# One code copy for the tokens of an expert beyond 512, behind all experts, in a kernel of attention, MLP and mixture of experts

## The chip, the cores and the metric

The kernel runs on one core of a Trainium2 chip, in one launch. Times are device microseconds (us) of that core. The kernel before takes 1265.66 us in the median of three runs (1262.17 to 1268.53). The engines are TensorE (PE in the profile; PEld is its weight load, which overlaps the matmuls), VectorE (DVE), ScalarE (ACT), GpSimd (POOL) and SyncE (SP). Each engine has its own instruction stream, and waits for others by semaphores. A branch stands in the stream of every engine, since all of them must go the same way.

## The reference, cut to what matters

Three stages follow each other on float32 data. The first is attention with batch 4, 8 heads, 576 positions and 64 columns a head, in which each query keeps its 32 largest scores:

```
scores = q @ k.T / 8
mask   = scores >= (32nd largest of the row)
attn   = softmax of the kept scores;  x = attn @ v       # 2304 tokens x 512
```

The second is a gated MLP with a root-mean-square norm, 512 to 1536 and back to 512:

```
xn = x / sqrt(mean(x*x) + 1e-6) * rms_g
x  = (silu(xn @ w_gate) * (xn @ w_val)) @ w_out
```

The third, which the change touches, is a mixture of 8 experts. Each token goes to the one expert with its largest logit:

```
logits = x @ w_gate + modality_bias[modality_id];  e_idx = argmax(logits)
gate_w = softmax(logits)[e_idx]
for e in range(8):                                    # tokens of expert e
    out[mask] = gate_w[mask] * (relu(x[mask] @ w1[e]) @ w2[e])   # 512 -> 1024 -> 512
```

How many tokens an expert gets is known only when the kernel has computed the logits. The weights of one expert are 4 MB, 32 MB for all.

## The kernel before, in words

The function front(False) holds attention, MLP and gate, some 930 us, in an order of steps written out by hand. It leaves three things: the rows x2_d in device memory, a table tab_d with the numbers and gate weights of each expert's tokens, and cnt_i, the eight counts. It also computes bad_i, a count of values outside the range in which the fast arithmetic holds; under "If bad > 0" (lines 1102 to 1103) the whole front is there again in exact arithmetic, and all engines jump over it. The last vector work before that is in verdict2 (lines 977 to 983), which writes cnt_i and bad_i.

Then come the experts, one after another (loop over e, from line 1262). The unit of work is 256 tokens (UNIT). For one unit

- gather (line 1135) reads 256 rows of the table (idx, six kept) and fetches the tokens' rows by an indirect DMA from POOL into xg, of which there are three buffers;
- columns (line 1146) transposes them on TensorE (line 1154, eight transposes a unit) and splits each value into a high part xh (ScalarE) and a low part xl (VectorE), as TensorE multiplies the rounded parts;
- hidden (line 1165) makes the first product, 8 blocks of 12 matmuls with 256 columns (lines 1177), and the ReLU, again split into hh and hl;
- emit (line 1220) makes the second product, two halves of 24 matmuls with 512 columns (line 1230), scales by the gate weight (line 1235) and scatters 128 rows at a time by an indirect DMA from POOL (line 1236).

One such unit has 32 matmuls xh times wh at line 1177. The weights come in pieces of 512 KB on SP's queue (load_piece, line 1115) and are split into high and low parts by ScalarE and VectorE (split, line 1125).

The first unit of an expert is always computed, also where it is not full. While it runs, the next expert's weights are loaded and split, and the next tokens gathered and transposed: the code asks for them at chosen points of hidden and emit (lists later, between, ahead). Behind it comes what depends on the count. "If counts > 256" (line 1289) holds the second unit, either whole or, where at most 128 tokens are left, as a half (line 1290, hidden_half at line 1189). "If counts > 512" (line 1294) holds a loop over all units beyond (line 1295), with its own gather, transposes, hidden and emit. It needs the expert's weights in the buffers, so it stands ahead of the next expert. Tokens of the next expert's first unit are gathered ahead of these branches.

The order of instructions on each engine is set when the program is built: a scheduler orders the instructions between two branches by a simulated time line. Nothing moves across a branch or across the end of an If or a loop, but the lists above let the next expert's work stand inside the present one's.

Of the kernel before, what the change touches and what calls it, by code (L numbers as in the profile page):

```python
# [20 lines left out]
def topk_attention_swiglu_moe_kernel(  # L21
# [97 lines left out]
    tok = const.tile([128, NB], I32, name="tok")  # L119
    cnt_i = const.tile([128, E], I32, name="cnt_i")  # L120
    bad_i = const.tile([128, 1], I32, name="bad_i")
    ssall = const.tile([128, NB], F32, name="ssall")


# [85 lines left out]
    def front(exact):  # L210
# [766 lines left out]
        def verdict2(pt, ones, b_):  # L977

            nc.tensor.matmul(out=pt[:, 16:16 + E], lhsT=ones16, rhs=acc_oh, start=True, stop=True)
            nc.vector.tensor_copy(cnt_i, pt[:, 16:16 + E])  # L980
            if not exact:
                nc.tensor.matmul(out=pt[:, 8:9], lhsT=ones, rhs=b_, start=True, stop=True)
                nc.vector.tensor_copy(bad_i, pt[:, 8:9])
# [151 lines left out]
    def gather(rows, queue=nc.gpsimd):  # L1135
        idx = up.tile([128, 2, 2], I32, name="idx", tag="idx", bufs=6)
        queue.dma_start(out=idx, in_=tab_d[rows, :].rearrange("(j p) t -> p j t", j=2))
        xg = up.tile([128, 2, DM], F32, name="xg", tag="xg", bufs=3)
        for j in range(2):
            last["gather"] = nc.gpsimd.indirect_dma_start(  # L1140
                out=xg[:, j, :], out_offset=None, in_=x2_d,
                in_offset=bass.IndirectOffsetOnAxis(ap=idx[:, j, 0:1], axis=0), bounds_check=NT, oob_is_err=False,
            )
        return idx, xg

    def columns(u):
        idx, xg = u
        xh = up.tile([128, KD, UNIT], F32R, name="xh", tag="xh", bufs=3)
        xl = up.tile([128, KD, UNIT], F32R, name="xl", tag="xl", bufs=3)
        for kk in range(0, KD, 2):  # L1150
            pt = ps_g.tile([128, 512], F32, name="pg")
            for a in range(2):
                for j in range(2):
                    nc.tensor.transpose(
                        pt[:, a * 256 + j * 128:a * 256 + (j + 1) * 128],
                        xg[:, j, (kk + a) * 128:(kk + a + 1) * 128], ident,
                    )
            pv = pt.rearrange("p (a n) -> p a n", a=2)
            nc.scalar.copy(out=xh[:, kk:kk + 2, :], in_=pv)
            nc.vector.tensor_tensor(  # L1160
                out=xl[:, kk:kk + 2, :], in0=pv, in1=xh[:, kk:kk + 2, :].bitcast(F32), op=OP.subtract
            )
        return idx, xh, xl

    def hidden(ws, u, between=()):
        idx, xh, xl = u
        between = list(between)
        hh = up.tile([128, KF2, UNIT], F32R, name="hh", tag="hh", bufs=1)
        hl = up.tile([128, KF2, UNIT], F32R, name="hl", tag="hl", bufs=1)
        for m in range(KF2):  # L1170
            pt = ps_h.tile([128, UNIT], F32, name="ph")
            n = 0
            for kk in range(KD):
                wh, wl = ws[kk]
                fs = slice(m * 128, (m + 1) * 128)
                for l, r in ((wh, xh), (wh, xl), (wl, xh)):
                    nc.tensor.matmul(out=pt, lhsT=l[:, fs], rhs=r[:, kk, :], start=(n == 0), stop=(n == 3 * KD - 1))  # L1177
                    n += 1
            a = nc.scalar.activation(out=hh[:, m, :], in_=pt, func=AF.Relu)  # L1179
            d = nc.vector.scalar_tensor_tensor(  # L1180
                out=hl[:, m, :], in0=pt, scalar=0.0, in1=hh[:, m, :].bitcast(F32), op0=OP.max, op1=OP.subtract
            )
            if between:
                with tc.issue_after(a.ins), tc.issue_after(d.ins):
                    for fn in between.pop(0):
                        fn()
        return idx, hh, hl
# [32 lines left out]
    def emit(ws, u, between=None, halves=2):  # L1220
        idx, hh, hl = u
        for j in range(halves):
            pt = ps_u.tile([128, 512], F32, name="pu")
            n = 0
            js = slice(j * 128, (j + 1) * 128)
            for f in range(KF2):
                wh, wl = ws[NPC + f // 2]
                ds_ = slice((f % 2) * DM, (f % 2 + 1) * DM)
                for l, r in ((hh, wh), (hh, wl), (hl, wh)):
                    nc.tensor.matmul(out=pt, lhsT=l[:, f, js], rhs=r[:, ds_], start=(n == 0), stop=(n == 3 * KF2 - 1))  # L1230
                    n += 1
            if j == 0 and between:
                between()
            o = up.tile([128, DM], F32, name="o", tag="o", bufs=2)
            nc.scalar.activation(out=o, in_=pt, func=AF.Copy, scale=idx[:, j, 1:2].bitcast(F32))  # L1235
            nc.gpsimd.indirect_dma_start(  # L1236
                out=out, out_offset=bass.IndirectOffsetOnAxis(ap=idx[:, j, 0:1], axis=0),
                in_=o, in_offset=None, bounds_check=NT - 1, oob_is_err=False,
            )
# [22 lines left out]
    for e in range(E):  # L1262
        more = e + 1 < E
        wn = []
        box = {}
        later = []
        for i in range(NPC):
            later.append([lambda i=i: split(ws[NPC + i])])
            if e == 0:
                later[i] += [lambda i=i: load_piece(wn, 1, 2 * i, nc.scalar), lambda i=i: load_piece(wn, 1, 2 * i + 1, nc.scalar)]  # L1270
        if more:
            with tc.issue_after(first) if e == 0 else ExitStack():
                g1 = gather(rows(e + 1, 0))
            if e > 0:
                for i in range(2 * NPC):
                    load_piece(wn, e + 1, i)
        later.append([lambda: box.update(c2=columns(g2))])

        def ahead():
            for w in wn[0:NPC]:  # L1280
                split(w)

        if more:
            later += [[]] * (KF2 - 1 - len(later)) + [[ahead]]
        emit(ws, hidden(ws, c1, later), (lambda: box.update(c1=columns(g1))) if more else None)
        c2, c1 = box["c2"], box.get("c1")
        if more:
            g2 = gather(rows(e + 1, 1))
        with tc.If(counts[e] > UNIT):
            with tc.If(counts[e] > UNIT + 128) as whole:  # L1290
                emit(ws, hidden(ws, c2))
            with whole.Else():
                emit(ws, hidden_half(ws, c2), halves=1)
        with tc.If(counts[e] > 2 * UNIT):  # L1294
            with tc.For_i(2 * UNIT, counts[e], UNIT) as i:
                emit(ws, hidden(ws, columns(gather(bass.ds(e * NT + i, UNIT)))))
        if more:
            ws = wn


# [31 lines left out]
```

## Time and profile before

| | |
|---|---|
| median of three runs | 1265.66 us |
| the profiled execution | 1265.35 us, its span 1263.7 us |
| mean granted clock of TensorE | 0.929 |
| TensorE matmuls, busy | 1140.6 us |
| VectorE, busy | 927.7 us |
| ScalarE, busy | 833.3 us |
| POOL, busy | 738.8 us |
| moved by DMA | 87.80 MB |

The profile is one execution. Its span runs from the first to the last record; the 1.65 us around it belong to the run's time. Busy time does not count branches, register loads, semaphores or the issue of a DMA: where an engine stands in a branch it is idle in these figures, and the engine's sequencer has an entry of its own (PEq, POOLq). Matmuls are handed over to TensorE ahead of time, so its sequencer can stand in a branch while earlier matmuls still run. The experts fill the last 325 us of the span. Times of the timeline are counted from the start of the span.

### The profile page before, as it was taken

The page shows a single profiled execution, that of the slowest core. Times are in us where ns is not written, and L with a number is a line of the kernel's source. Part 1 is how long each engine was busy: PE and PEld are TensorE (multiplying, and loading weights), DVE is VectorE, ACT ScalarE, POOL GpSimd, SP SyncE. Part 2 cuts the span into 40 slices and gives each one's busy share as a digit, 9 for nine tenths or more (in the row PEclk, how much of TensorE's full clock was granted, in tenths as well). Part 3 has the DMA queues.
Part 4 walks back from the last instruction along what each step waited for, and adds up shares of the span by engine and source line. Part 5 has one row for each costly group of instructions (what it writes and reads, how often), then busy time and mean ns, then how long its engine had stood idle before and what let it go on. Part 6 is the DMA issues. An engine that isn't in the chain of part 4 may idle for free. (4 is left out here: it accounts for less than half of the span.)

```text
span 1263.7 us, 32277 instructions
## 1 busy us (share of the span) xinstructions
PE 1140.6 (90%) x12286; PEld 1044.3 (83%) x12286; DVE 927.7 (73%) x2883; ACT 833.3 (66%) x1757; POOL 738.8 (58%) x850
## 2 busy tenths in 40 slices
PE   6976777989999999999999999999948898999985
PEld 6965667988999999999898999999937897798884
DVE  7999999669999999999999999921115434254251
ACT  5868888677888888888998788753315434354251
POOL 7866767668857888777798767643423222022120
PEclk9856677989999999999999999999978998999998
DMA  8143312011000111000011000000029525354130
GB/s 289 51 126 84 96 44 79 14 45 48 9 17 17 28 40 53 17 8 18 23 38 40 17 15 10 2 11 19 2 71 348 185 73 209 109 184 139 70 116 18
DMA packets 68894, 87.80 MB, mean 69 GB/s; under 512 B 34386, under 2 KB 43734, under 8 KB 68696
## 3 DMA queue, kind: packets, MB, share of 16 engines
q1 hardware_dynamic: 60152, 63.66, 16.3%
q0 software_dynamic: 6320, 16.31, 3.8%
q10 hardware_dynamic: 2224, 5.25, 1.2%
q8 instruction: 117, 1.92, 0.7%
q14 instruction: 81, 0.66, 0.2%
HBM read 75.58 MB, written 10.92 MB: 68 GB/s over the span
## 5 line engine op out<-in xcount | busy, mean ns | idle before, releaser
L561 DVE MAX8 w<-w 128x8 f32<-128x296 f32 x576 | 249.8, 456 | 1.2
L595 POOL TENSOR_TENSOR s<-s,r 128x576 f32<-128x576 f32 x144 | 201.2, 1419 | 31.8 <-ACT r L591 31.5
L564 DVE MATCH_REPLACE8 w<-w 128x296 f32<-128x296 f32 x432 | 193.1, 449 | 0.0
L746 PE MATMUL pf<-xT,wg 128*128 128x128 f16 (+1 forms) x2448 | 172.5, 224 | 5.0 <-DVE T L875 2.9
L746 PE MATMUL pf<-xT,wv 128*128 128x128 f16 (+1 forms) x2448 | 168.8, 223 | 0.3 <-ACT xf L735 0.3
L746 PEld LDWEIGHTS <-wg 128*128 128x128 f16 x2448 | 148.8, 99 | 11.4 <-issue 5.4
L746 PE MATMUL po<-wo,h 128*128 128x264 f16 (+1 forms) x1296 | 157.4, 275 | 0.9 <-ACT t L773 0.9
L526 PE MATMUL ps<-kS,qS 128*128 128x288 f32 x640 | 138.4, 345 | 21.2 <-DVE w L542 20.3
L746 PEld LDWEIGHTS <-wv 128*128 128x128 f16 x2448 | 146.5, 98 | 4.6 <-issue 0.4
L746 PEld LDWEIGHTS <-h 128*128 128x128 f16 x1296 | 121.9, 98 | 18.8 <-issue 1.4
L1236 POOL DMA_INDIRECT out_dram<-o,idx x23 | 22.8, 993 | 195.7 <-ACT o L1235 139.6
L1180 DVE SCALAR_TENSOR_TENSOR hl<-ph,hh 128x256 fp32r<-128x256 f32 x88 | 36.9, 421 | 132.0 <-ACT hh L1179 129.0
L526 PEld LDWEIGHTS ps<-kS,qS 128*128 128x128 f32 x640 | 103.9, 215 | 24.4 <-ACT r L591 14.8
L599 ACT ACTIVATE s<-s,mbs 128x576 f32<-128x576 f32 x144 | 113.3, 788 | 13.5 <-POOL s L595 13.1
L1177 PE MATMUL ph<-xh,wh 128*128 128x256 f32 x352 | 101.5, 291 | 16.4 <-PEq L1294 16.0
L591 ACT ACTIVATE r<-s,mbs 128x576 f32<-128x576 f32 x144 | 104.9, 779 | 13.9 <-POOL mbs L582 13.8
L621 PE MATMUL pt<-identr,s 128*128 128x128 f32 x576 | 98.2, 302 | 14.8 <-ACT s L599 13.7
L539 ACT COPY s<-ps 128x576 f32<-128x576 f32 x144 | 93.2, 647 | 21.8 <-PE ps L526 21.2
L1177 PE MATMUL ph<-xl,wh 128*128 128x256 f32 x352 | 100.3, 286 | 0.0
L1177 PE MATMUL ph<-xh,wl 128*128 128x256 f32 x352 | 100.3, 286 | 0.0
L778 POOL TENSOR_TENSOR t<-u,t 128x512 f32<-128x512 f32 x54 | 69.6, 1290 | 48.1 <-ACT t L773 28.8
L667 PE MATMUL pt<-vs,pT 128*128 128x64 f16 (+1 forms) x1680 | 88.4, 198 | 8.7 <-POOL pT L635 6.0
(204 smaller groups left out, 2825.1 us busy)
## 6 DMA issues: line engine op xcount, KB each, us to landing
wr<-in_moe_w_dram SPq DMA_DIRECT2D x48, 512.0 KB
wst<-in_moe_w_gate_dram SPq DMA_DIRECT2D x24, 256.0 KB
wst<-in_moe_w_val_dram SPq DMA_DIRECT2D x24, 256.0 KB
wr<-in_moe_w_dram ACTq DMA_DIRECT2D x10, 512.0 KB
kr<-in_k_dram SPq DMA_DIRECT2D x32, 128.0 KB
vt<-in_v_dram SPq DMA_DIRECT2D x32, 128.0 KB
x_d<-xo SPq DMA_DIRECT2D x16, 256.0 KB
qr<-in_q_dram SPq DMA_DIRECT2D x112, 32.0 KB
```

Of the source, the lines that this page charges most:

```text
L526: nc.tensor.matmul(out=ps[:, a, 0:HS], lhsT=qS[i // 2][:, i % 2, j, o2:o2 + 128], rhs=kt[:, m, ks], start=(n == 0), stop=(n == len(ops) - 1),)
L539: nc.scalar.copy(out=s.rearrange("p (a k) -> p a k", a=2), in_=ps[:, :, 0:HS])
L561: steps.append(lambda: dve.max(lists[t][:, 8 * r:8 * r + 8], src[t] if r == 0 else dst[t]))
L564: steps.append(lambda: dve.match_replace(out=dst[t], in_to_replace=lists[t][:, 8 * r:8 * r + 8], in_values=src[t] if r == 0 else dst[t], i ...
L591: nc.scalar.activation(out=d["r"], in_=d["s"], func=AF.Relu, scale=-BIG, bias=d["mb"][:, 1:2])
L595: nc.gpsimd.tensor_tensor(out=d["s"], in0=d["s"], in1=d.pop("r"), op=OP.subtract)
L599: nc.scalar.activation(out=d["s"], in_=d["s"], func=AF.Exp, scale=SCALE, bias=d["mb"][:, 0:1], accum_out=d["rs"])
L621: nc.tensor.transpose(pt[:, c * 128:(c + 1) * 128], e[:, e0 + c * 128:e0 + (c + 1) * 128], ident)
L667: nc.tensor.matmul(out=av_[o:o + n], lhsT=l, rhs=r, start=(a == 0), stop=(a == len(ops) - 1))
L746: nc.tensor.matmul(out=out_, lhsT=l, rhs=r, start=(a == 0), stop=(a == len(ops) - 1))
L778: nc.gpsimd.tensor_tensor(out=t, in0=u, in1=t, op=OP.mult)
L1177: nc.tensor.matmul(out=pt, lhsT=l[:, fs], rhs=r[:, kk, :], start=(n == 0), stop=(n == 3 * KD - 1))
```

## The change

The loop over the units beyond 512 leaves the body of the loop over the experts. It is written again behind all experts: a new register holds the largest of the eight counts, and under one branch on it each expert with more than 512 tokens has its weights loaded and split again and its loop run. The largest count comes from a maximum and a cast on VectorE, ahead of bad_i in verdict2. The branches at 256 tokens stay. Lines behind the insertions have higher numbers in the new program: by 2 up to line 980, by 4 from there to the new code.

```diff
--- before.py
+++ after.py
@@ -119,6 +119,8 @@
     tok = const.tile([128, NB], I32, name="tok")
     cnt_i = const.tile([128, E], I32, name="cnt_i")
     bad_i = const.tile([128, 1], I32, name="bad_i")
+    most_f = const.tile([128, 1], F32, name="most_f")
+    most_i = const.tile([128, 1], I32, name="most_i")
     ssall = const.tile([128, NB], F32, name="ssall")
 
 
@@ -978,6 +980,8 @@
 
             nc.tensor.matmul(out=pt[:, 16:16 + E], lhsT=ones16, rhs=acc_oh, start=True, stop=True)
             nc.vector.tensor_copy(cnt_i, pt[:, 16:16 + E])
+            nc.vector.tensor_reduce(out=most_f, in_=pt[:, 16:16 + E], axis=AX.X, op=OP.max)
+            nc.vector.tensor_copy(most_i, most_f)
             if not exact:
                 nc.tensor.matmul(out=pt[:, 8:9], lhsT=ones, rhs=b_, start=True, stop=True)
                 nc.vector.tensor_copy(bad_i, pt[:, 8:9])
@@ -1291,11 +1295,22 @@
                 emit(ws, hidden(ws, c2))
             with whole.Else():
                 emit(ws, hidden_half(ws, c2), halves=1)
-        with tc.If(counts[e] > 2 * UNIT):
-            with tc.For_i(2 * UNIT, counts[e], UNIT) as i:
-                emit(ws, hidden(ws, columns(gather(bass.ds(e * NT + i, UNIT)))))
         if more:
             ws = wn
+
+    most = nc.values_load(
+        most_i[0:1, 0:1], min_val=0, max_val=NT, skip_runtime_bounds_check_because="a count of tokens"
+    )
+    with tc.If(most > 2 * UNIT):
+        for e in range(E):
+            with tc.If(counts[e] > 2 * UNIT):
+                ws = []
+                for i in range(2 * NPC):
+                    load_piece(ws, e, i)
+                for w in ws:
+                    split(w)
+                with tc.For_i(2 * UNIT, counts[e], UNIT) as i:
+                    emit(ws, hidden(ws, columns(gather(bass.ds(e * NT + i, UNIT)))))
 
 
 # ---- launch: one core; inputs and outputs as the reference has them ----
```

The scheduler can now order instructions where the loop's branches stood before. Three places show it. The first is TensorE's stream where expert 0 ends: its second unit, the loop and the start of expert 1. "pg" is the result of a transpose, "ph" of the first product, "pu" of the second. Before:

```order
L1230 MATMUL pu<-wh,hl 128x512
L1290 UNCONDITIONAL_BRANCH
L1289 UNCONDITIONAL_BRANCH
L1294 COMPARE_AND_BRANCH
L1295 COMPARE_AND_BRANCH
L1295 UNCONDITIONAL_BRANCH x2
L1327 BRANCH_PREFETCH_HINT
L1154 MATMUL pg<-identr,xg 128x128 x8
L1177 MATMUL ph<-xh,wh 128x256 x4
```

After:

```order
L1234 MATMUL pu<-wh,hh 128x512
L1234 MATMUL pu<-wl,hh 128x512
L1234 MATMUL pu<-wh,hl 128x512
L1294 UNCONDITIONAL_BRANCH
L1293 UNCONDITIONAL_BRANCH
L1181 MATMUL ph<-xh,wh 128x256
L1181 MATMUL ph<-xl,wh 128x256
```

The loop with its branches and the body (transposes and two products) has left this place; the first matmul of the next expert follows the end of the second unit. A block from the count's load of one expert to that of the next was 492 rows of this list without weight loads, and is 346.

The second place is the end of expert 0's first unit on TensorE, ahead of the load of its count. Before:

```order
L1230 MATMUL pu<-wh,hl 128x512
L1230 MATMUL pu<-wh,hh 128x512
L1230 MATMUL pu<-wl,hh 128x512
L1230 MATMUL pu<-wh,hl 128x512
L1245 TENSOR_LOAD cnt_i
L1289 COMPARE_AND_BRANCH
```

After:

```order
L1234 MATMUL pu<-wh,hh 128x512
L1234 MATMUL pu<-wl,hh 128x512
L1234 MATMUL pu<-wh,hl 128x512
L1158 MATMUL pg<-identr,xg 128x128 x8
L1249 TENSOR_LOAD cnt_i
L1293 COMPARE_AND_BRANCH
```

The eight transposes of the next expert's tokens, which stood among the matmuls of the second product, now stand behind all of them. In the other experts this part of TensorE's stream is the same as before.

The third place is POOL's stream behind the second unit of expert 0, with expert 1's first unit. "idx" is a read of the table, "xg" a gather, "out_dram" a scatter. Before:

```order
L1294 ISA
L1294 UNCONDITIONAL_BRANCH
L1137 DMA idx<-tab_d 128x2x2 x2
L1140 DMA xg<-x_d,idx 128x512 x4
L1236 DMA out_dram<-o,idx 2304x512 x2
L1245 TENSOR_LOAD cnt_i
```

After:

```order
L1293 ISA
L1293 UNCONDITIONAL_BRANCH
L1141 DMA idx<-tab_d 128x2x2 x2
L1144 DMA xg<-x_d,idx 128x512 x2
L1240 DMA out_dram<-o,idx 2304x512
L1144 DMA xg<-x_d,idx 128x512 x2
L1240 DMA out_dram<-o,idx 2304x512
L1249 TENSOR_LOAD cnt_i
```

The second pair of gathers now stands between the two scatters, and these gathers are for tokens one unit later than before: expert 0's part has two units more of them. SP's stream is unchanged up to the end. At the end every engine loads the new register and jumps over eight copies of the loop (on POOL the code from there to the last barrier is 132 rows of this list).

## Rows read from the trace of the kernel before

**Rows 1.** The page's busy times, and its group of xh times wh.

```profile
PE 1140.6 (90%) x12286; PEld 1044.3 (83%) x12286; DVE 927.7 (73%) x2883; ACT 833.3 (66%) x1757; POOL 738.8 (58%) x850
...
L1177 PE MATMUL ph<-xh,wh 128*128 128x256 f32 x352 | 101.5, 291 | 16.4 <-PEq L1294 16.0
```

**Rows 2.** Windows: stretch, length, busy by engine, granted clock, DMA share, GB/s.

```profile
core 0: us, PE busy (x) PEld busy (x) DVE busy (x) ACT busy (x) POOL busy (x), PEclk, DMA share, GB/s
1196.20:1220.30 24.10, 24.05 (x160) 21.69 (x160) 14.68 (x20) 13.86 (x22) 8.37 (x8) 1.00 0.44 149
1060.80:1064.80 4.00, 3.95 (x18) 3.98 (x19) 0.42 (x1) 0.96 (x2) 1.68 (x3) 0.50 0.06 7
1088.70:1092.00 3.30, 3.22 (x8) 2.60 (x9) 0.00 (x0) 0.00 (x0) 0.48 (x1) 0.51 0.23 84
1225.20:1229.00 3.80, 3.80 (x22) 3.80 (x21) 2.08 (x3) 2.25 (x4) 0.00 (x0) 0.55 0.00 0
1105.10:1121.80 16.70, 16.70 (x125) 15.62 (x124) 12.94 (x18) 11.87 (x19) 6.01 (x7) 1.00 0.66 219
```

**Rows 3.** TensorE's timeline at borders: start, us, [idle before <-releaser].

```profile
983.50 0.55 PE L1177 MATMUL ph<-xh,wh 128*128 128x256 f32 x1 [5.66 <-PEq L1294]
...
1030.40 0.40 PE L1230 MATMUL pu<-wh,hl 128*128 128x512 f32 x1
1031.10 0.36 PE L1177 MATMUL ph<-xh,wh 128*128 128x256 f32 x1 [0.30 <-PEq L1294]
...
1054.55 0.39 PE L1230 MATMUL pu<-wl,hh 128*128 128x512 f32 x1
...
1054.78 0.40 PE L1230 MATMUL pu<-wh,hl 128*128 128x512 f32 x1
1060.85 0.55 PE L1177 MATMUL ph<-xh,wh 128*128 128x256 f32 x1 [5.67 <-PEq L1294]
...
1088.78 0.77 PE L1201 MATMUL pu<-wh,xh 128*128 128x512 f32 x1 [1.97 <-issue]
...
1223.79 0.36 PE L1177 MATMUL ph<-xh,wh 128*128 128x256 f32 x1 [3.45 <-PEq L1294]
```

**Rows 4.** Line 1294 by queue: ns least/median/most, first and last start.

```profile
L1294 DVEq COMPARE_BRANCH  x8: 56/56/69, 976.5 to 1238.9; - x8
...
L1294 PEldq COMPARE_BRANCH  x8: 374/3194/3397, 979.9 to 1249.1; - x8
```

**Rows 5.** Single branches on TensorE's queue, lines 1289 and 1294.

```profile
L1289 PEldq COMPARE_BRANCH  x1: 5619/5619/5619, 974.1 to 974.1; - x1
...
L1289 PEldq COMPARE_BRANCH  x1: 5747/5747/5747, 1051.3 to 1051.3; - x1
...
L1294 PEldq COMPARE_BRANCH  x1: 3256/3256/3256, 1057.3 to 1057.3; - x1
...
L1289 PEldq COMPARE_BRANCH  x1: 3664/3664/3664, 1216.5 to 1216.5; - x1
```

**Rows 6.** DMA queues, 1105.0 to 1122.5 us: packets, MB, share of 16 engines.

```profile
q8 instruction: 2, 0.03, 0.7%
```

**Rows 7.** TensorE's timeline at transposes of gathered tokens.

```profile
949.41 1.54 PE L1154 MATMUL pg<-identr,xg 128*128 128x128 f32 x6 [2.26 <-DMA xg<-x_d,idx]
...
1038.00 1.04 PE L1154 MATMUL pg<-identr,xg 128*128 128x128 f32 x8
```

**Rows 8.** VectorE's timeline, the cast to bad_i.

```profile
928.99 0.16 DVE L983 CAST bad_i<-pv 128x1 int32<-128x1 f32 x1 [0.47 <-PE pv L982]
```

**Rows 9.** POOL's queue at the end, 1245 to 1264 us.

```profile
L1289 POOLq INC_SWDGE_SEM  x1: 2048/2048/2048, 1250.4 to 1250.4; - x1
...
L1245 POOLq TENSOR_LOAD <-cnt_i x1: 292/292/292, 1249.8 to 1249.8; - x1
...
L1327 POOLq DRAIN  x3: 46/108/7752, 1255.1 to 1263.5; - x3
```

**Rows 10.** POOL's queue at line 1103, the branch over the exact front.

```profile
L1103 POOLq EVENT_SEMAPHORE  x5: 17/43/43, 935.5 to 935.9; - x5
L1103 POOLq COMPARE_BRANCH  x1: 45/45/45, 929.8 to 929.8; - x1
```

## The prediction

> **What bounds the kernel now.** The page comes first: TensorE is busy for 90% of the span, VectorE for 73% [rows 1]. The change touches only the last quarter, the eight experts, so the stretches come next: the stretch of expert 6's tokens has TensorE busy for 24.05 of 24.10 us, and VectorE and ScalarE for under 15 [rows 2]. There TensorE sets the time, and a microsecond in which it stands still is lost. Third, the timeline of TensorE, read for idle time at the borders between experts [rows 3]. There are two kinds. After an expert whose second 256 tokens were computed (1, 3, 4, 5) the next matmul starts 0.30 us after the last one ended. After an expert whose second 256 were skipped (0, 2, 6) TensorE is idle for 5.66, 5.67 and 3.45 us, and the profile names its own sequencer at line 1294, the branch of the loop that the change moves.
>
> Fourth, the branches themselves [rows 4]. On VectorE the branch at line 1294 takes 56 ns. On TensorE's queue it takes 3194 ns in the median of eight, once 374. The loop ran for nobody: xh times wh ran 352 times [rows 1], which is 11 units of 32, eight first units and the three full second ones of experts 1, 4 and 5 (expert 3 took the half). So all eight branches jumped over a body, and such a jump costs TensorE about 3.2 us.
>
> Rows 5 show when that is paid. At expert 2 the branch of line 1289 starts at 1051.3 and takes 5.75 us; the last matmul, already handed over, runs until 1055.18, so 3.9 us of the jump are covered. The branch of line 1294 follows at 1057.3 for 3.26 us with nothing left to cover it, and the next matmul starts at 1060.85. At expert 6 the first jump takes 3.66 us from 1216.5 and is covered whole; the second is bare, and 3.45 us stay idle [rows 3]. At experts 1, 4 and 5 the loop's jump is the one behind the queue of matmuls, and it is covered.
>
> **What a jump is made of.** TensorE's instructions come over their own DMA queue in blocks: two fetches of together 0.03 MB, one at each end of the stretch from 1105.1 to 1121.8 us [rows 6], in which TensorE does 124 or 125 pairs of weight load and matmul [rows 2]. So one block is about 16 KB and lasts about 128 pairs. A jump that leaves the blocks already there has to fetch. At expert 6, whose successor's weights are all loaded (DMA 0.00 after the border [rows 2]), that takes 3.66 us, at experts 0 and 2 5.62 and 5.75 [rows 5].
>
> **The change part by part**, against the profiled execution's 1265.35 us (span 1263.7), which stands 0.3 us below the median of 1265.66.
>
> *Expert 6 to 7.* The loop's jump goes; the first one ends at 1220.2, when the last matmul still runs. What is left is the kind of 0.30 us that the taken borders show: 3.45 − 0.30 = 3.15 us. [...] Together 4.85.
>
> *Expert 2 to 3.* If the first jump keeps its 5.75 us, the gap falls from 5.67 to about 2.2 (the 3.26 and 0.2 of semaphore work go), 3.45 us, and the clock still drops: around the 1.97 us gap at line 1201 it was at 0.51 for 3.3 us [rows 2, 3], so only 4.0 − 3.3 us at half clock return, 0.4. That is 3.8, the lower end. But two loop bodies ahead of this branch are gone, and the place of the jump in its block moves. I count 200 pairs of jump, 1.6 blocks, and by the two dated blocks the branch now stands about 0.2 of a block behind a block's start, so that its target lies in the next block, whose fetch was sent off some 25 pairs (over 5 us) earlier. This is an estimate. The one loop branch that cost 374 ns shows that such a place exists. Then the gap is 0.30 and the clock holds: 5.67 − 0.30 = 5.37, and half of the 4.0 us, 2.0, together 7.35. I take that, the upper end, since the count is the nearer evidence, and keep 3.8 in the range.
>
> [...]
>
> *Expert 0 to 1.* The first jump keeps its place (nothing ahead of it on TensorE moves in or out) and its 5.62 us. What is ahead of it is reordered: the eight transposes of the next tokens now stand last. Eight of them take 1.04 us [rows 7] where eight matmuls of 512 columns take 1.84 (0.23 each, from the starts in rows 3), so the cover of 3.7 us shrinks to 2.9 and the gap is 5.62 − 2.9 + 0.3 = 3.0. Saved: 2.65. Ends: 2.0 if the copies behind the transposes are late as well, 3.45 if the cover holds.
>
> *Experts 1, 3, 4, 5.* The semaphore work of the skipped branch, which waits until TensorE has emptied, goes. From start to start the border costs 0.70 us where a matmul costs 0.23 [rows 3]. I take 0.4 each, 1.6 in all; ends 0 and 1.9.
>
> *POOL and SP.* The gathers move up by one expert, and POOL's own work at the loop's branch goes. In the new order one gather stands between the two scatters of an expert and waits for the transposes of the expert's successor; those run between the two halves of the second product, so the second scatter, which needs the later half, is not held up. I count nothing; it is hidden under TensorE, which has 24.05 busy us where POOL has 8.37 [rows 2]. If a gather came late that cover would be gone, see the rivals. SP's order is the same.
>
> *Start.* The maximum and its cast are two small VectorE instructions ahead of bad_i, for which all engines wait. One of them stands in the chain: 0.16 us by the next cast [rows 8], between 0 and 0.4 (both, and the semaphore between them).
>
> *End.* Behind the last scatter POOL still does one INC_SWDGE_SEM of 2.05 us, then a load of the new register (0.29), the jump over all eight loops and, as today, its drain of 7.75 us [rows 9]. The new jump is long on every engine. The nearest long jump is at line 1103: POOL's own branch is over in 45 ns at 929.8, yet its next instruction comes at 935.5 [rows 10], 5.7 us with the other engines fetching as well. Bounds: 0.05 if the code is there, and 5.7; I take 3.0, a little under TensorE's median of 3.19 [rows 4], since the engines are idle by then and no weights are in flight. With the load 3.3 us later.
>
> **Sum:** −4.85 − 7.35 − 2.65 − 1.6 + 0.16 + 3.3 = −13.0, so 1265.35 − 13.0 = 1252.3 us.
>
> **The rivals.**
> *Expert 2's jump keeps its price* (the block count is off): −13.0 + 3.55 = −9.45, 1255.9 us. For it: the jumps at experts 0 and 2 both cost 5.6 us or more today [rows 5].
> *The end is cheaper and expert 3 gains too.* If POOL's drain swallows the late start, 3.0 us come back; the jump into expert 3's half, with 1.97 us idle [rows 3], moves as well, up to 1.97 − 0.30 = 1.7 us: 1265.35 − 17.7 = 1247.6. Against it: nothing shows what the drain waits for.
> *A branch costs only its own instruction*, the gaps being time for the code that follows, which has to be fetched in any case. Then the removed branches are worth what VectorE pays, 8 × 0.056 = 0.4 us [rows 4], and the time is 1264.9. [...] Against the rival: at expert 2 the wait is two jumps end to end, 5.75 and 3.26, and the loop's jump at expert 3 took 374 ns although the same code followed.
> *Slower: the gathers on POOL become the wait.* TensorE waits 2.26 us for a gather at the start of the experts, with weights in flight [rows 7]. If the new order made each of eight experts wait so, 18 us would be added to the −13.0: 1270.4. It decides where a gather lands after its transposes are due; the change issues gathers earlier, not later, so the chance is small.
> *The change does not do what it says:* the tail runs, and an expert's 4 MB are loaded again. The loop ran for nobody [rows 1] and the inputs are the same, so I give it nothing.
>
> **How the numbers follow.** A measurement of this kernel can tell 0.5% (6.3 us) from no change. Chances: the forecast 0.42, expert 2's jump as before 0.28, the cheap end 0.15, the branch alone 0.10, slower 0.05. The smaller bounds add up to 5.0 us against me (expert 0 at 2.0 costs 0.65, the four borders at nothing 1.6, an end of 5.7 adds 2.7); expert 2's jump as before, with all of these, is 1260.9, so I put 0.06 of its 0.28 to no change. That makes faster 0.42 + 0.22 + 0.15 = 0.79, within 0.5% 0.16, slower 0.05. The runs shown differ by 3 us from their median; the range reaches from 1245, below the cheap end, to 1261, that worst case of expert 2's jump, and leaves out the last two cases.
>
> **What would show it.** In the profile of the changed kernel no branch of TensorE stands between two experts but those of the second 256 tokens, and the idle time ahead of the first matmul is about 3 us after expert 0, 0.3 after 2 and 6. The granted clock does not fall after expert 6. If expert 2 shows about 2.2 us, its jump kept its price. At the end POOL's next instruction after the new branch comes some 3 us later. The prediction is wrong if the gaps stay at 5.7 us under another line's name, if TensorE waits for gathers between experts, or if the time from the last scatter to the end grows by as much as the gaps shrink.

## The result and the profile after

The changed kernel takes 1253.68 us in the median of four runs (1253.03 to 1254.91), the kernel before 1267.1 us in the median of four (1262.17 to 1269.27). The ratio is 0.9894, with a 95% interval of 0.9873 to 0.9915: faster by 1.1%. The forecast was 1252.3. The profiled execution took 1253.59 us, its span is 1251.9 us, 11.8 less than before, so the two profiles can be compared piece by piece.

The page's groups first, for the matmuls of [rows 1]. Idle time ahead of them falls from 16.4 to 6.8 us, and the mean of one from 291 to 288 ns, which is the clock: one takes 281 ns in the mean where the granted clock is 1.00 and 433 to 434 where it is 0.50, in both traces, and 22 of the 352 stood at 0.50 before, 14 after.

```profile
PE 1134.4 (91%) x12286; PEld 1038.2 (83%) x12286; DVE 925.4 (74%) x2885; ACT 832.3 (66%) x1757; POOL 736.2 (59%) x850
...
L1181 PE MATMUL ph<-xh,wh 128*128 128x256 f32 x352 | 100.2, 288 | 6.8 <-PEq L1293 6.3
```

TensorE's timeline at the borders, as in [rows 3]: the first matmuls of experts 1, 3 and 7, and expert 3's half.

```profile
985.84 0.55 PE L1181 MATMUL ph<-xh,wh 128*128 128x256 f32 x1 [5.74 <-PEq L1293]
...
1058.55 0.36 PE L1181 MATMUL ph<-xh,wh 128*128 128x256 f32 x1 [0.30 <-PEq L1293]
...
1082.46 0.39 PE L1205 MATMUL pu<-wh,xh 128*128 128x512 f32 x1
...
1211.39 0.36 PE L1181 MATMUL ph<-xh,wh 128*128 128x256 f32 x1 [0.30 <-PEq L1293]
```

Expert 2's 5.67 us and expert 6's 3.45 have become 0.30. Expert 0's 5.66 is 5.74. The 1.97 us ahead of expert 3's half are gone, a gain that the forecast had only in a rival. The branches that explain this stand on TensorE's queue, to be read beside [rows 5] (experts 0, 2 and 6; line 1293 is the old 1289). Expert 0's jump takes 6.46 us where it took 5.62, expert 2's has gone from 5.75 us to 0.37, and expert 6's is about as long as it was and covered as it was:

```profile
L1293 PEldq COMPARE_BRANCH  x1: 6456/6456/6456, 979.1 to 979.1; - x1
...
L1293 PEldq COMPARE_BRANCH  x1: 365/365/365, 1054.4 to 1054.4; - x1
...
L1293 PEldq COMPARE_BRANCH  x1: 3587/3587/3587, 1207.2 to 1207.2; - x1
```

The branch into expert 3's half (line 1290, now 1294), before and after: it takes 2.85 us in place of 5.54 and ends at 1081.74, while TensorE still has matmuls of the first unit to do, so it is covered.

```profile
L1290 PEldq COMPARE_BRANCH  x1: 5542/5542/5542, 1083.1 to 1083.1; - x1
```

```profile
L1294 PEldq COMPARE_BRANCH  x1: 2851/2851/2851, 1078.9 to 1078.9; - x1
```

The windows behind these borders, columns as in [rows 2]. Where TensorE stood still for 0.30 us the clock is at 1.00, behind the 5.74 us at 0.50 for 5 us.

```profile
985.80:990.80 5.00, 4.96 (x23) 5.00 (x24) 1.06 (x2) 1.32 (x2) 2.31 (x3) 0.50 0.13 28
1058.50:1062.50 4.00, 3.95 (x35) 3.98 (x36) 1.32 (x2) 2.73 (x5) 1.02 (x1) 1.00 0.28 89
...
1211.30:1215.20 3.90, 3.81 (x33) 3.84 (x34) 1.18 (x2) 2.63 (x5) 0.97 (x1) 1.00 0.14 48
```

The end on POOL's queue, to be read beside [rows 9] (lines 1301 and 1304 are the load of the largest count and its branch). The branch takes 45 ns at 1238.4, yet the next instruction of POOL comes at 1241.0, 2.6 us later. A second INC_SWDGE_SEM and the drain of 7.75 us follow. The kernel before has a second INC_SWDGE_SEM too, of expert 7's loop branch, which [rows 9] do not show (the last line here), so the new one adds nothing to the difference.

```profile
L1301 POOLq TENSOR_LOAD <-most_i x1: 298/298/298, 1238.0 to 1238.0; - x1
...
L1304 POOLq EVENT_SEMAPHORE  x2: 43/43/43, 1241.0 to 1241.1; - x2
L1304 POOLq COMPARE_BRANCH  x1: 45/45/45, 1238.4 to 1238.4; - x1
L1304 POOLq INC_SWDGE_SEM  x1: 2051/2051/2051, 1241.2 to 1241.2; - x1
...
L1342 POOLq DRAIN  x3: 46/103/7752, 1243.3 to 1251.6; - x3
```

```profile
L1294 POOLq INC_SWDGE_SEM  x1: 2036/2036/2036, 1253.1 to 1253.1; - x1
```

All of the time in one table, worked out from the timelines of the profiled executions: "front" is the start of the last matmul of the verdict, "first" the time from there to expert 0's first product, e0 to e6 run from an expert's first matmul to that of the next, e7 to the end of the last matmul, "end" from there to the end of the span.

```
              front   first   e0     e1     e2     e3     e4     e5     e6     e7     end     span
before        928.70  22.33  32.46  47.60  29.75  42.88  46.26  46.27  27.53  25.15  14.79  1263.73
after         930.41  22.98  32.44  48.40  24.31  36.72  46.07  45.74  24.31  23.18  17.31  1251.88
no tail       929.16  21.12  31.58  48.13  24.31  36.74  45.74  45.74  24.31  23.19  12.05  1242.07
near loop     931.29  21.44  32.52  48.62  26.62  36.81  46.06  45.82  24.88  23.36  12.55  1249.97
held          941.31  19.86  28.96  45.88  24.31  36.73  46.07  45.74  24.37  23.18  17.83  1254.23
pad 90        927.96  23.46  28.39  46.08  26.64  36.72  46.07  45.74  24.31  23.18  17.87  1246.42
pads both     926.46  22.79  28.11  45.81  24.31  36.74  45.74  45.74  24.31  23.19  17.26  1240.44
one branch    927.75  21.05  27.97  50.32  24.15  38.33  45.82  45.83  24.14  23.02  12.33  1240.69
one br., 20   929.73  21.03  28.62  49.11  24.16  36.97  45.73  45.58  24.40  23.27  12.32  1240.90
best          930.30  21.06  27.35  45.89  24.14  36.60  45.72  45.58  24.40  23.01  12.34  1236.39
pad 43        930.57  23.96  30.85  48.10  27.24  38.35  45.74  45.74  24.31  23.19  17.28  1255.34
```

"front" moves from 926 to 931 us between builds whose matmuls have the same order (all but "held"). One kernel's executions scatter as much (no tail by 5.1 us, pad 43 by 8.7), so a median alone does not settle a difference of 2 or 3 us. From expert 1 on, an expert's time repeats to about 0.5 us where nothing about it is changed; expert 0's does so only to 1.6 (32.44, 31.58 and 30.85 us in the changed kernel, no tail and pad 43, all with the same order and a long jump). So theories of single borders are told apart in this table.

### The profile page after: what moved, and what is told of

Its sections match the earlier page's. It is cut to its first block, busy times and chain, and to the rows that moved or that the text cites. A ratio compares the mean times of both kernels' runs of the same rounds, so it can differ in the third digit from the quotient of the medians.

```text
span 1251.9 us, 32217 instructions
## 1 busy us (share of the span) xinstructions
PE 1134.4 (91%) x12286; PEld 1038.2 (83%) x12286; DVE 925.4 (74%) x2885; ACT 832.3 (66%) x1757; POOL 736.2 (59%) x850
```

## The experiments

Theory J: what costs is a jump on TensorE to code that has to be fetched, and its price depends on where in its block the jump and the target lie. The rivals: B, the branch itself costs, wherever it leads; and, for expert 0, C, the order of the transposes took the cover. Places in a block ("by the count") are estimates, from the order of TensorE's instructions and the 124 or 125 pairs of weight load and matmul that [rows 2] show between the two fetches of [rows 6].

The traces show what a long jump waits for. Within expert 0's jump in the changed kernel, 979.0 to 985.6 us, one block comes over the instruction queue of [rows 6]. Within expert 2's, 1054.4 to 1054.8, the one queue that moves anything is that of the weights.

```profile
q8 instruction: 1, 0.02, 1.0%
```

```profile
q1 hardware_dynamic: 43, 0.16, 108.9%
```

The same holds in all eleven kernels of the table, from 925 us on. Of TensorE's 151 compare branches of up to 0.44 us none has the start of a block's fetch within it. Of the 57 that take 1.6 us or more, 54 have one, and the other three begin 0.01, 0.2 and 1.2 us behind the start of one. At the experts such a branch ends 2.3 to 3.1 us behind the fetch's start. The rest of its price is the time until the fetch starts: 4.1 us at expert 0 here, 1.1 at expert 6. Where it is 2.4 us or more the DMA engines' share is 0.76 to 1.04 over it, but in one kernel (one branch, 20; expert 3) it is 1.1 us at a share of 1.05. Why a fetch starts late stays open.

**No tail.** The changed kernel without the code at the end and without the maximum; tokens beyond 512 are left out.

```diff
-            nc.vector.tensor_reduce(out=most_f, in_=pt[:, 16:16 + E], axis=AX.X, op=OP.max)
-            nc.vector.tensor_copy(most_i, most_f)
...
-    with tc.If(most > 2 * UNIT):
...
```

> The changed kernel without the code behind the experts and without the maximum and its cast; tokens beyond 512 are left out (there are none in these inputs). Theory J (a jump to code that has to be fetched costs): POOL's next instruction after its last branch comes at once, the time from the last scatter's issue to the end falls from 16.2 to about 13.7 us, the rest stays: 1251.1 us. Rival: the drain at the end waits for something that is as late as before, so nothing comes back: 1253.7. For the two small VectorE instructions: if they cost anything, the time from the first matmul of the verdict to the cast of bad_i is shorter than 1.63 us; by the trace of the changed kernel it stays at 1.63.

Measured: 1247.91 us, ratio 0.9852 [0.9828, 0.9875]. POOL's queue at the end: one INC_SWDGE_SEM, and the drain follows at once.

```profile
L1291 POOLq INC_SWDGE_SEM  x1: 2040/2040/2040, 1231.4 to 1231.4; - x1
```

```profile
L1326 POOLq DRAIN  x3: 46/103/7749, 1233.5 to 1241.8; - x3
```

The end takes 12.05 us in place of 17.31, so the branch there costs 5.3 us and not 2.6: besides the wait of 2.6 a second INC_SWDGE_SEM of 2.05, the load of 0.30 and some 0.4 of waits. The expectation had counted the fetch alone. The drain starts later by all of it, so it swallows nothing. The two VectorE instructions cost nothing: from the verdict's first product to the cast of bad_i it takes 1.63 us before, after and here.

**Near loop.** The kernel before, its loop in place with a small body.

```diff
-                emit(ws, hidden(ws, columns(gather(bass.ds(e * NT + i, UNIT)))))
+                z = up.tile([128, DM], F32, name="o", tag="o", bufs=2)
+                nc.vector.memset(z[:, 0:1], 0.0)
```

> The kernel before with the loop where it was, branch and all, but with a body of one small VectorE memset, so that the jump over it is short; tokens beyond 512 are left out. Theory J (the distance of the jump costs): the branch of the loop takes at most 0.5 us on TensorE at all eight experts, and the idle time after expert 6 is about 0.7 us. Expert 2's first jump lies at the edge of its block: 0.4 us, or 5.6. Without a jump at the end (2.6 us less than the changed kernel) and with some 0.35 us for each small loop: 1253.8 us, or 1257 where expert 2's jump misses. Rival B (the branch itself, its semaphores and the emptying of TensorE cost): still some 3 us of TensorE's queue at the loop's branch and about 1265 us.

Measured: 1249.29 us, 0.9865 [0.984, 0.9889]. All eight branches on TensorE's queue in one row, against a median of 3194 ns in [rows 4]:

```profile
L1294 PEldq COMPARE_BRANCH  x8: 207/344/2172, 984.9 to 1237.7; - x8
```

The branches are there, their semaphores too, and seven of eight cost 0.2 to 0.4 us. That is against B. The idle time after expert 6 is 0.79 us (0.7 expected). The eighth, expert 2's with 2.17 us, broke the expectation of 0.5; a block's fetch starts 0.2 us ahead of it, and by the count it is the one whose target lies just behind a block's edge (the first jump of 0.34 us lands just ahead of it), where the expectation had put the risk on the first jump. The median is 4.5 us under the forecast of 1253.8, mostly because the end is 4.8 us shorter than the changed kernel's and not 2.6, and "first" 1.5 shorter (table). Without a loop body in the way the gathers moved as in the changed kernel, and expert 0 has the same late transposes.

**Held.** The changed kernel with expert 2's gathers behind expert 0's first scatters.

```diff
-            with tc.issue_after(first) if e == 0 else ExitStack():
+            with tc.issue_after(first) if e == 0 else tc.issue_after(held) if e == 1 else ExitStack():
                 g1 = gather(rows(e + 1, 0))
...
+        if e == 0:
+            held = last["scatter"].ins
...
+            with tc.issue_after(held) if e == 1 else ExitStack():
                 g2 = gather(rows(e + 1, 1))
```

> The changed kernel with the gathers for expert 2 held behind expert 0's first scatters, which gives expert 0 TensorE's order of the kernel before (its transposes among the matmuls and not behind them). Theory C (the matmuls handed over ahead cover part of the jump, and the wait ahead of the late transposes took that cover): the idle time between experts 0 and 1 falls from 5.74 to about 2.2 us and the clock is low for less time behind it: 1249.5 us. Rival: the order has nothing to do with it, the jump of 6.5 us is bare anyhow: 1253.7.

Measured: 1256.1 us, 0.9917 [0.9894, 0.994], against the forecast of 1249.5. The edit also made the scheduler order the whole front anew, from its 58th matmul on, and the verdict's product starts at 941.18, 11 us later than after. The border itself did what C says:

```profile
L1296 PEldq COMPARE_BRANCH  x1: 5096/5096/5096, 984.7 to 984.7; - x1
```

```profile
990.13 0.35 PE L1181 MATMUL ph<-xh,wh 128*128 128x256 f32 x1 [1.65 <-PEq L1296]
```

The jump still takes 5.1 us, the idle time is 1.65 in place of 5.74, and experts 0 and 1 are 6.0 us shorter (table). The branch starts at 984.72 and the last matmul ahead of it ends at 988.48, a cover of 3.76 us, as before. As a version it is useless, and its median says nothing on C (it is nearer to the rival's 1253.7); the border speaks for C.

**Pad 90.** Code that is never executed moves all code behind it. In the traces of pads 90, 43 and both, TensorE, VectorE, ScalarE and POOL do the same instructions in the same order as in the changed kernel.

```diff
     with tc.If(bad > 0):
         front(True)
+        with tc.tile_pool(name="padp", bufs=1, space=PSUM) as pp:
+            pd = pp.tile([128, 512], F32, name="pd")
+            for _ in range(90):
+                nc.tensor.matmul(out=pd[:, 0:128], lhsT=ident16, rhs=ones16, start=True, stop=True)
```

> The changed kernel with 90 matmuls that are never executed, in the exact front that all engines jump over. They shift TensorE's code behind by 180 instructions, 0.7 of a block, and change nothing that runs. Theory J with blocks (the place of a jump in its block decides): expert 0's jump now ends in the next block and takes about 0.4 us in place of 6.5, and the clock behind it holds, 7.9 us less; expert 2's jump no longer does and takes about 5.6 us, with an idle time of 2 us and a lower clock behind it, 3.6 us more: 1249.4 us. Rival (the place makes no difference; expert 2's gap went because the loop's branch went): expert 0 idle for 5.7 us, expert 2 for 0.3, 1253.7 us.

Measured: 1250.38 us, 0.9877 [0.9854, 0.9901]. The jumps of experts 0 and 2 have changed places, as the count said:

```profile
L1297 PEldq COMPARE_BRANCH  x1: 442/442/442, 977.0 to 977.0; - x1
...
L1297 PEldq COMPARE_BRANCH  x1: 6103/6103/6103, 1046.0 to 1046.0; - x1
```

TensorE's timeline at the two borders: expert 0's idle time is 1.85 us (now VectorE's queue ends it, no longer TensorE's: the copies of the late transposes are the wait that is left), expert 2's is 2.63.

```profile
979.80 0.36 PE L1185 MATMUL ph<-xh,wh 128*128 128x256 f32 x1 [1.85 <-DVEq L1297]
...
1052.53 0.36 PE L1185 MATMUL ph<-xh,wh 128*128 128x256 f32 x1 [2.63 <-PEq L1297]
```

Experts 0 and 1 gain 6.4 us, expert 2 loses 2.3. The clock did not fall behind the 2.63 us, which the expectation had assumed: it is 1.00 in the window behind that border (columns as in [rows 2]), and expert 3 keeps its 36.72.

```profile
1052.50:1056.50 4.00, 3.97 (x35) 4.00 (x36) 1.35 (x2) 2.28 (x4) 0.99 (x2) 1.00 0.13 47
```

**Pad 43.** The same with 43 matmuls.

> The changed kernel with 43 never executed matmuls in the exact front: TensorE's code lies 86 instructions, 0.34 of a block, further on. By the count the jumps of experts 0, 2 and 7 all end two blocks on, expert 6's lies at an edge. Theory J with blocks: expert 0 stays at 5.7 us idle, expert 2's gain is lost again: its branch takes about 6 us, TensorE is idle for 2.6 us there and the expert takes 26.7 us in place of 24.3: 1256.0 us. Rival (the change itself freed expert 2): 24.3 us, 1253.7.

Measured: 1254.32 us, 0.9922 [0.9898, 0.9946]. The six executions reach from 1248.37 to 1257.04 (the profiled one), so the median does not decide between the 1256.0 expected and the rival's 1253.7; the border does. Expert 0 is idle for 5.43 us (5.7 expected). Expert 2's jump:

```profile
L1297 PEldq COMPARE_BRANCH  x1: 6734/6734/6734, 1053.7 to 1053.7; - x1
```

```profile
1060.72 0.36 PE L1185 MATMUL ph<-xh,wh 128*128 128x256 f32 x1 [3.22 <-PEq L1297]
```

```profile
1060.70:1066.70 6.00, 5.98 (x38) 6.00 (x39) 2.24 (x4) 2.64 (x4) 1.51 (x2) 0.72 0.18 37
```

The expert takes 27.24 us in place of 24.31, and here the clock behind the border falls (0.72 over the next 6 us), which costs expert 3 another 1.6. The loop's branches stand at the end here too, as in the changed kernel. So about half of what expert 2 gained by the change (2.3 and 2.9 of 5.44 us in the two runs) is the place that its first jump happened to get.

**Pads both.** Pad 90, and 50 matmuls in expert 1's half, which expert 1 does not execute.

```diff
             with whole.Else():
                 emit(ws, hidden_half(ws, c2), halves=1)
+                if e == 1:
+                    pd = ps_g.tile([128, 512], F32, name="pg")
+                    for _ in range(50):
+                        nc.tensor.matmul(out=pd[:, 0:128], lhsT=ident16, rhs=ones16, start=True, stop=True)
```

> The changed kernel with two sets of matmuls that are never executed: 90 in the exact front, as in the run before, and 50 in expert 1's half, which expert 1 jumps over. By the count of blocks the jumps of experts 0 and 2 both end in the next block. Theory J with blocks: expert 0 as in the run with 90 (4.1 us less, and 2.3 us less in expert 1 from the clock), expert 2 as in the changed kernel (0.3 us idle), expert 3's jump into its half at most partly late and covered: 1253.7 - 6.4 = 1247.3 us. Rival (the place in the block makes no difference, and the run with 90 was a swap of something else between experts 0 and 2): expert 2's idle time stays at 2.6 us, 1250.4.

Measured: 1247.24 us, 0.985 [0.983, 0.987]. Both jumps are short, and the border after expert 2 is at 0.30 us again:

```profile
L1297 PEldq COMPARE_BRANCH  x1: 442/442/442, 974.5 to 974.5; - x1
...
L1297 PEldq COMPARE_BRANCH  x1: 353/353/353, 1043.3 to 1043.3; - x1
```

```profile
1047.47 0.36 PE L1185 MATMUL ph<-xh,wh 128*128 128x256 f32 x1 [0.30 <-PEq L1297]
```

**One branch.** The code for more than 512 tokens ahead of the experts, in the branch that all engines jump over anyway.

```diff
+                nc.vector.scalar_tensor_tensor(
+                    out=rare_i, in0=most_f, scalar=2.0 * UNIT, in1=pt[:, 8:9], op0=OP.subtract, op1=OP.max
+                )
...
+    with tc.If(rare > 0):
...
+        with tc.If(bad > 0):
+            front(True)
...
+        with tc.If(most > 2 * UNIT), ExitStack() as stack:
...
```

> The code for tokens beyond 512 stands neither in the loop nor at the end but ahead of the experts, inside the branch over the exact front: that one branch is now taken where values are out of range or an expert has more than 512 tokens, by one more VectorE instruction, and holds two branches for the two cases. All is computed. Theory J: a jump over both costs TensorE and the others what the jump over the exact front cost before (5 to 6 us on TensorE's queue), the end is as without the code there (1247.9 us), and 0.2 us go to the VectorE instruction. TensorE's code lies 0.9 of a block further on: expert 0's jump ends in the next block (6.4 us less with the clock behind it), expert 3's jump into its half does not (some 3 us more): 1244.7 us. If expert 0's jump, which by my count ends 0.04 of a block ahead of the edge, misses: 1251. Rival (a longer jump costs more): the first gather comes later by some us than in the other runs.

Measured: 1241.87 us, 0.9808 [0.9787, 0.983]. On TensorE's queue the longer jump costs no more than the shorter one (5.18 us, where the jump over the exact front takes 5.49 before and 5.42 after), and the end is that of "no tail" to 0.3 us (table):

```profile
L1103 PEldq COMPARE_BRANCH  x1: 5491/5491/5491, 929.8 to 929.8; - x1
```

```profile
L1107 PEldq COMPARE_BRANCH  x1: 5424/5424/5424, 931.5 to 931.5; - x1
```

```profile
L1260 PEldq COMPARE_BRANCH  x1: 5184/5184/5184, 928.8 to 928.8; - x1
...
L1325 PEldq COMPARE_BRANCH  x1: 442/442/442, 973.9 to 973.9; - x1
...
L1326 PEldq COMPARE_BRANCH  x1: 4802/4802/4802, 1071.7 to 1071.7; - x1
```

Expert 0's jump is short, expert 3's into its half is long, as expected; expert 2's takes 2.99 us and is covered. But expert 1 takes 50.3 us. The timeline shows a second stop, a few matmuls behind the border:

```profile
976.76 0.36 PE L1174 MATMUL ph<-xh,wh 128*128 128x256 f32 x1 [1.85 <-DVEq L1325]
979.90 0.37 PE L1174 MATMUL ph<-xh,wl 128*128 128x256 f32 x1 [1.60 <-issue]
```

The clock then is 0.50 for 5 us. By the count the jump's target lies 0.04 of a block ahead of the edge, so the code would run out a few matmuls later. The trace bears that out: a block's fetch starts at 977.59, between the border and the stop (the instruction queue from 977.5 to 979.9 us), and TensorE goes on 2.31 us behind it, as behind the long jumps (2.3 to 3.1).

```profile
q8 instruction: 1, 0.02, 2.6%
```

The median is 2.8 us under the forecast of 1244.7 although this stop was not in it: "front" and "first" are 4.6 us shorter than in the changed kernel (table).

**One branch, 20.** With 20 matmuls in expert 1's half.

> The run before with 20 matmuls that are never executed in expert 1's half, so that by the count expert 3's jump into its half ends in the next block and expert 2's still does. Theory J with blocks: no idle time ahead of expert 3's half, 3 us less than the run before, 1241.7 us. Rival: no difference between the two.

Measured: 1242.32 us, 0.9808 [0.9788, 0.9827]. Expert 3 loses its stop (36.97 us in place of 38.33), expert 1 keeps its own (49.11). But the jump into expert 3's half is not free, as the expectation had it: it still waits for a fetch, 3.46 us in place of 4.80, and is covered.

```profile
L1326 PEldq COMPARE_BRANCH  x1: 3464/3464/3464, 1073.1 to 1073.1; - x1
```

The total does not show the 1.4 us; the 3 of the expectation were too many.

**Best.** 109 matmuls inside the branch and 38 in expert 1's half.

> The kernel with one branch ahead of the experts for both rare cases, with 109 never executed matmuls inside that branch and 38 in expert 1's half. By the count of blocks the jumps of experts 0 and 2 end in the next block, at 0.8 of it, and no longer at 0.96, and expert 3's jump into its half starts at 0.1 of a block. Theory J with blocks: no idle time of 1.4 to 1.6 us a few matmuls behind the border of experts 0 and 1 (there the next block was asked for only when the jump landed), the clock behind it holds, expert 1 takes 45.8 us as in the run with two pads and not 49 to 50: 1239.0 us, 3.3 less than the run with 20. Rival: the idle time there has another cause (gathers, weights) and stays: 1242.3.

Measured: 1238.67 us, 0.9801 [0.9777, 0.9826]. The stop behind the border is gone, and expert 1 takes 45.89 us. The window of 9 us behind that border, of this kernel and of "one branch", columns as in [rows 2]:

```profile
978.70:987.70 9.00, 8.99 (x79) 9.00 (x80) 6.37 (x10) 6.74 (x11) 2.59 (x3) 1.00 0.80 270
```

```profile
976.70:985.70 9.00, 7.34 (x39) 7.28 (x40) 3.30 (x4) 2.91 (x5) 3.83 (x5) 0.62 0.62 201
```

79 matmuls at 1.00 against 39 at 0.62. The jump into expert 3's half takes 2.94 us and is covered. This version computes everything that the kernel before computes and beats both kernels: 2.0% under the kernel before, and under the changed one by 15 us by the medians, 12 by the ratios. Its rare branch ran in no run, since no expert here has more than 512 tokens.

## Why the prediction came out right, step by step

**Expert 6** was right in mechanism and size: 3.22 us of the border (3.15 forecast), and 1.97 us of expert 7 by the clock (1.7). The 1.7 in its 4.85 are an estimate from [rows 2]: 3.8 us at a clock of 0.55, of which 0.45 come back. Behind the border of 0.30 us the clock is 1.00, where the forecast had it.

**Expert 2** was right: 5.44 us (5.37), and 1.9 of the clock behind it (2.0; expert 3's first 60 matmuls take 7.06 us at a mean clock of 1.00 where they took 8.94 at 0.78). The chosen end, that the first jump goes free by its new place in a block, is what pads 90 and 43 confirm: move the place and the jump is back at 6.1 and 6.7 us. The fetch that the forecast put some 25 pairs ahead of the branch starts at 1048.56 in the trace, 29 matmuls and 5.8 us ahead. That such a jump goes free or waits for a fetch is what these runs show: the first jumps of experts 0 and 2 take, behind the change and in the experiments, 0.34 to 0.44 us where by the count the target lies in the next block, 5.1 to 6.7 where it lies two blocks on, each of these with a fetch in it, and once 2.99, in "one branch", where the fetch starts 0.5 us behind the branch.

**Expert 0** is the step that failed. It forecast "the cover of 3.7 us shrinks to 2.9" and a jump that keeps its 5.62 us, 2.65 us saved. Measured: the cover shrank to 1.04 us (the branch starts at 979.06, the last transpose ends at 980.09), the jump took 6.46 us, nothing was saved, and expert 1 took 0.8 longer by the clock (0.50 for 5 us behind the border, where it was 0.53 for 3). Of the 2.7 us that are missing at this border, 1.9 are the cover and 0.8 the longer jump, whose fetch starts 4.1 us behind the branch in place of 2.9; why is open. The transposes stand last, and the forecast counted their length, not their wait. The timelines of VectorE and TensorE there:

```profile
973.89 3.49 DVE L1133 TENSOR_TENSOR wl<-wr,wh 128x1024 fp32r<-128x1024 f32 x3
977.30 1.28 DVE L1164 TENSOR_TENSOR xl<-pg,xh 128x512 fp32r<-128x512 f32 x2
```

```profile
978.60 0.19 PEld L1234 LDWEIGHTS pu<-wh,hl 128*128 128x128 f32 x1
978.83 0.59 PEld L1158 LDWEIGHTS pg<-identr,xg 128*128 128x128 f32 x4
```

VectorE splits weights until 977.4 and reads the first transposes' results until 978.58. Only then are their two buffers free for the next eight, and TensorE's queue, held at them, has nothing handed over ahead but these when it comes to the branch. In each of the nine kernels with the late transposes the branch starts 0.48 or 0.49 us behind VectorE's last read; in the kernel before and in "held" it starts over 6 us behind it. The prediction's own lower end (2.0, "if the copies behind the transposes are late as well") comes nearest to this wait, and priced it too low. "Held" shows that with the old order most of the jump is covered again.

**Experts 1, 3, 4, 5:** 0.2 and 0.5 us at experts 4 and 5 (0.4 forecast). Expert 3 gained 6.2 in all: 1.9 of the clock, 2.0 of the stop ahead of its half, 1.65 as the half ran at full clock (5.66 us at 1.00 in place of 7.31 at 0.77), the rest at its border. The forecast had the first and the last; the stop stood in a rival as a move of the jump. It did move, but not out of a fetch: its fetch starts 0.5 us behind the branch in place of 3.2, so the jump takes 2.85 us and is covered. With the code moved by pads 90, 43 and both, the same jump takes 0.35 us, so its price depends on the place too; what makes the fetch start earlier in the changed kernel was not tried apart. Expert 1 had 0.4 in the forecast and lost the 0.8 named above.

**Start:** 0.16 forecast, 0 found. The 1.7 us by which the front was longer stand ahead of the added instructions and lie in its scatter. The gathers behind it were 0.65 us later; why that piece varies from 19.9 to 24.0 us between builds (table) was not tried.

**End:** 3.3 forecast, 2.5 measured. POOL's wait behind the new branch is 2.6 in place of 3.0; and the 0.45 us that it spent behind the loop's branch of expert 7 went, which the forecast did not count.

The sum was −13.0 and came out as −11.85 in the spans (−13.4 by the two medians of four). Expert 0 and the clock behind it missed 3.5 us, the start 2.2 more, and expert 3's half gave back 3.6, the end 0.8. Right in size, then, partly because errors met.

Of the rivals, "a branch costs only its own instruction" is refuted by "near loop": a branch of the same line takes 0.34 us there in the median, where it took 3.19 over the body. "The gathers become the wait" did not come: no border shows TensorE waiting for a gather. One sentence of the section on the kernel before was too strong: instructions do move across an If. POOL's gathers for expert 2 now stand ahead of expert 0's branch. In "near loop" they do so too and the transposes are as late; in "held" they are kept behind the scatters and the transposes stand among the matmuls again.

## What to carry to other kernels

In these kernels TensorE sets the time in the experts, and a branch over code that never ran was paid for when its target had to be fetched: the first jumps of experts 0 and 2 took 2.99 to 6.7 us of TensorE's queue with a fetch in them, and 0.34 to 0.44 without. So count the instructions from jump to target and estimate where blocks begin, and look at the branch's own duration on that engine's queue and for a fetch within it. Put rare code where a jump is taken anyway (one jump over both rare cases took 5.18 us on TensorE's queue, that over one of them 5.42), or where other work covers it (expert 6's jump of 3.59 us left 0.30 idle), and not behind the last useful instruction (5.3 us). When an edit moves much code and borders far from it change, shift the code by something that never runs before you believe a story about the edit: here such a shift took back 2.3 and 2.9 us of expert 2's 5.44.

## What the runs showed that was not expected

- The branch at the end cost a whole 5.3 us on POOL, two fifths of it one INC_SWDGE_SEM of 2.05 us.
- In "one branch" a jump of 0.44 us that waited for no fetch was followed by a stop of TensorE, 1.60 us, eleven matmuls later, with a block's fetch ahead of it that started at 977.59; by the count the jump had landed at the end of a block.
- The clock was at 0.51 behind a stop of 1.97 us in the kernel before and held at 1.00 behind one of 2.63 us in pad 90; the length of a stop alone does not tell it.
